# Two weight copies on TensorE, each made three times, ahead of the stream of matmuls

## The chip, the cores and the metric

One core of a Trainium2 chip. The time is the device time of one execution in microseconds; medians are given with the lowest and highest run. The profile's span is about 1.7 us shorter than that time. Only one core ran, so there is no second die to compare with; all timed runs used here are classed as fast, except the one single look (`pauses`), whose state is unknown.

## The reference, cut to what matters

```python
H = W = 384; C = 384; k = 1
x: (1, 384, 384, 384) bf16, dw: (1, 1, 384) bf16, pw: (384, 384) bf16
out = x * dw[0, 0]                          # k = 1: a scale per channel
return einsum('bhwc,cd->bhwd', out, pw)     # 147456 x 384 times 384 x 384
```

The scale is folded into the weights: `w_r = diag(dw) pw`, made once on the chip, and then one long product.

## The kernel before: the parts concerned

In the head, TensorE runs filler matmuls of zeros (`idle_work`), then makes the scaled and reordered weights. For each 128-row block `k` and half `r` it multiplies `pw_n` by a scaled selection matrix into PSUM (a pair of 64-row matmuls, `v` = 0, 1); ScalarE or VectorE copies each result to `w_r` in SBUF. I call such a pair "the copy (k, r)". Then comes the stream: 288 supertiles of 512 positions and 48 matmuls. VectorE transposes the input into `T`; each supertile uses four PSUM banks, and ScalarE copies them to `O`.

```python
idle_work(1)                              # 4 matmuls of zeros; idle_work(3) comes earlier
for k in range(3):
    if k < 2:
        nc.tensor.wait_ge(s_pw[k], 16)    # weights landed
    nc.tensor.wait_ge(s_sw, k + 1)
    for r in range(2):
        if k == 2:
            nc.tensor.wait_ge(*w_done[r]) # these PSUM banks are read out
        for v in range(2):
            mm = nc.tensor.matmul(PS[(k + 1) % 2][:, 2 * r + v, :D],
                lhsT=sel_w[64 * v : 64 * v + 64, k, r, :, :]...,
                rhs=pw_n[64 * v : 64 * v + 64, k, :],
                start=True, stop=True, tile_position=(64 * v, 0))
        mm.then_inc(s_w)
with nc.tensor.Fori(0, NS // 2, 1) as it:  # the stream
    ...                                    # first matmul waits for the third ScalarE copy of w_r
# ... cut
for t, (g, i, off, first, L) in enumerate(chunks):   # one queue for loads and stores
    todo.append((g_end[g - NR] if g >= NR else -1, load_x, t))
    todo.append((first + L + 1, store, t))
```

## Time and profile before

| | before |
|---|---|
| time, three runs | 576.89 us (576.73 to 577.27) |
| TensorE busy | 568.2 us, 99% of the span |
| stream starts | 6.47 us |
| one stream matmul, first supertile / rest of the run | 519 / 321 ns |
| first copy of outputs, last copy of outputs start | 10.54, 570.50 us |
| VectorE, ScalarE busy | 88%, 73% |

It is read from the end backwards: TensorE holds the chain, its stream has no idle time after the start, so the time is the start of the stream, plus the stream, plus a tail of stores. The lines themselves are in the prediction.

### The profile page before, as it was taken

What the parts mean: (1) busy time and instruction counts of PE and PEld (TensorE: products, weight loads), DVE (VectorE), ACT (ScalarE), POOL (GpSimd) and SP (SyncE); (2) the same over time, 40 slices, a digit from 0 to 9 for tenths busy, and PEclk for the clock granted to TensorE, in tenths of its full rate; (3) what the DMA queues carried; (4) which work ended last, traced back from release to release, by engine and by line L of the source; (5) the groups of instructions that cost most, each with busy time, mean ns of one, the idle gap of its engine ahead of it and who ended that gap; (6) DMA issues with size and microseconds to landing.
All of it is one profiled execution on the core that took longest, in us unless ns stands there. A gap on an engine that the chain in (4) does not pass through costs nothing.

```text
span 575.2 us, 29676 instructions
## 1 busy us (share of the span) xinstructions
PE 568.2 (99%) x13855; PEld 386.4 (67%) x13855; DVE 507.4 (88%) x583; ACT 418.8 (73%) x296; POOL 0.9 (0%) x8
## 2 busy tenths in 40 slices
PE   8999999999999999999999999999999999999996
PEld 4666666666666666666666666666666666666664
DVE  6889888988898889888988898889888988898884
ACT  5777777777777777777777777777777777777775
POOL 0000000000000000000000000000000000000000
PEclk9999999999999999999999999999999999999999
DMA  8999999999999999999999999999999999994996
GB/s 346 425 399 415 436 411 429 426 419 386 383 436 397 383 392 426 399 394 398 427 404 385 400 431 387 388 421 420 385 394 420 399 394 401 413 400 169 416 385 240
DMA packets 25928, 226.88 MB, mean 394 GB/s; under 512 B 1213, under 2 KB 5694, under 8 KB 22078
## 3 DMA queue, kind: packets, MB, share of 16 engines
q1 hardware_dynamic: 25916, 226.79, 98.0%
q14 instruction: 9, 0.07, 0.0%
q8 instruction: 1, 0.02, 0.0%
q10 hardware_dynamic: 2, 0.00, 0.0%
HBM read 113.54 MB, written 113.25 MB: 394 GB/s over the span
## 4 chain that ended last, share of the span: by engine, by line
PE 98%; ACT 1%; DMA 0%; DVE 0%; issue 0%; POOL 0%; POOLq 0%; SPq 0%
PE ps L167 97%; DMA out_dram<-O 0%; ACT w_r L271 0%; ACT O L307 0%; PE ps L184 0%; DVE O L304 0%; PE ps L216 0%; DVE sel_w L286 0%; POOL zero L232 0%; DVE dw_f L283 0%; POOL warm L231 0%; PE ps L199 0%; POOLq L337 0%; SPq L100 0%
## 5 line engine op out<-in xcount | busy, mean ns | idle before, releaser
L167 PE MATMUL ps<-w_r,T 32*128 32x384 bf16 x13824 | 564.0, 322 | 0.5 <-ACT w_r L271 0.5
L258 DVE STREAM_TRANSPOSE T<-X 128x384 uint32<-128x384 uint32 x576 | 504.2, 876 | 57.9 <-PE ps L167 1.2
L307 ACT CAST O<-ps 128x1536 bf16<-128x1536 f32 x288 | 413.6, 1436 | 149.9 <-PE ps L167 149.9
L167 PEld LDWEIGHTS ps<-w_r,T 32*128 32x128 bf16 x13824 | 385.1, 93 | 179.4 <-issue 0.9
L271 ACT CAST w_r<-ps 128x768 bf16<-128x768 f32 x5 | 3.6, 820 | 1.0 <-PE ps L216 1.0
L304 DVE CAST O<-ps 128x768 bf16<-128x768 f32 x1 | 1.0, 958 | 3.0 <-DMA out_dram<-O 3.0
L184 PE MATMUL ps<-zero 32*128 32x384 bf16 x16 | 1.8, 494 | 1.4 <-POOL zero L232 1.4
L216 PE MATMUL ps<-pw_n,sel_w 64*128 64x384 bf16 x12 | 2.4, 507 | 0.3 <-DVE sel_w L286 0.3
L244 ACT ACT_TABLE_LOAD x1 | 1.3, 1283 | 1.5 <-SPq L100 1.5
L216 PEld LDWEIGHTS ps<-pw_n,sel_w 64*128 64x128 bf16 x12 | 0.7, 109 | 2.0 <-DMA pw_n<-in_pw_dram 1.0
L276 DVE TENSOR_REDUCE sel<-eye 128x64 f32<-128x128 bf16 x1 | 0.3, 290 | 1.8 <-POOL eye L234 1.8
L184 PEld LDWEIGHTS ps<-zero 32*128 32x128 bf16 x16 | 0.5, 99 | 2.0 <-issue 2.0
L271 DVE CAST w_r<-ps 128x768 bf16<-128x768 f32 x1 | 1.0, 958 | 0.5 <-PE ps L216 0.5
L286 DVE TENSOR_SCALAR sel_w<-sel,dw_f 128x256 bf16<-128x256 f32 x3 | 0.9, 351 | 0.0
L283 DVE COPY dw_f<-ps 128x3 f32<-128x3 f32 x1 | 0.2, 160 | 0.8 <-PE ps L199 0.8
L199 PEld LDWEIGHTS ps<-ones,dw_row 1*128 1x128 bf16 x3 | 0.2, 99 | 0.2 <-issue 0.2
L234 POOL TENSOR_SCALAR_AFFINE_SELECT eye<-ones 128x128 bf16<-128x128 bf16 x1 | 0.3, 292 | 0.1
L244 ACT COPY warm<-warm 128x1 f32<-128x1 f32 x2 | 0.3, 189 | 0.0
L232 POOL MEMSET zero<- 128x192 uint32 x1 | 0.3, 258 | 0.0
L199 PE MATMUL ps<-ones,dw_row 1*128 1x1 bf16 x3 | 0.2, 160 | 0.0
L233 POOL MEMSET ones<- 128x128 bf16 x1 | 0.2, 204 | 0.0
L326 POOL MEMSET const-bfloat16-1.0<- 128x1 bf16 x1 | 0.1, 102 | 0.0
(4 smaller groups left out, 0.4 us busy)
## 6 DMA issues: line engine op xcount, KB each, us to landing
X<-in_x_dram SPq DMA_DIRECT2D x26, 3840.0 KB, 20.9
out_dram<-O SPq DMA_DIRECT2D x26, 3840.0 KB, 26.9
X<-in_x_dram SPq DMA_DIRECT2D x2, 1536.0 KB, 16.6
out_dram<-O SPq DMA_DIRECT2D x2, 1536.0 KB, 13.2
X<-in_x_dram SPq DMA_DIRECT2D x3, 768.0 KB, 7.3
out_dram<-O SPq DMA_DIRECT2D x3, 768.0 KB, 11.4
X<-in_x_dram SPq DMA_DIRECT2D x1, 2304.0 KB, 18.7
out_dram<-O SPq DMA_DIRECT2D x1, 2304.0 KB, 11.0
```

The costliest lines, as they stand in the source:

```text
L167: mm = nc.tensor.matmul(PS[s][:, q, :D], lhsT=Ts[s][32 * q : 32 * q + 32, b, par::2], rhs=w_r[32 * q : 32 * q + 32, b, par, :], start=(b, ...
L184: nc.tensor.matmul(PS[0][:, i, :D], lhsT=zero[32 * i : 32 * i + 32, 0:P], rhs=zero[32 * i : 32 * i + 32, :], start=True, stop=True, tile_p ...
L199: mm = nc.tensor.matmul(PS[1][:, 0, D + k : D + k + 1], lhsT=dw_row[:, P * k : P * k + P], rhs=ones[0:1, 0:1], start=True, stop=True,)
L216: mm = nc.tensor.matmul(PS[(k + 1) % 2][:, 2 * r + v, :D], lhsT=sel_w[64 * v : 64 * v + 64, k, r, :, :].rearrange("p q w -> p (q w)"), rhs ...
L232: nc.gpsimd.memset(zero[:].bitcast(U32), 0).then_inc(s_zero)
L234: nc.gpsimd.affine_select(out=eye[:], in_=ones[:], pattern=[[-1, P]], compare_op=mybir.AluOpType.is_equal, fill=0.0, base=0, channel_multi ...
L244: c = nc.scalar.copy(warm[:, s + 1 : s + 2], warm[:, 0:1])
L258: ins = nc.vector.transpose(out=Tw[:, 3 * h : 3 * h + 3], in_=Xw[:, :, j, 96 * h : 96 * h + 96].rearrange("p k (b w) -> p b k w", w=32),)
L271: o = nc.vector.tensor_copy(out, in_) if e == 0 else nc.scalar.copy(out, in_)
L286: nc.vector.tensor_scalar_mul(sel_w[:, k], sel[:].unsqueeze(2).to_broadcast([P, 2, 4, 32]), dw_f[:, k : k + 1]).then_inc(s_sw)
L304: e = nc.vector.tensor_copy(Ov[:, nq:4, j, :], PS[s][:, nq:4, :D])
L307: a = nc.scalar.copy(Ov[:, 0:nq, j, :], PS[s][:, 0:nq, :D])
```

## The change

The intent, as I read it, is to keep TensorE busy up to the first matmul of the stream. The copies (1, 1) and (2, 0) are issued three times. Each repeat writes the same product to the same banks again; the semaphore is raised after the last.

```diff
         idle_work(1)
+        times = {(1, 1): 3, (2, 0): 3}
         for k in range(3):
...
-                for v in range(2):
+
+                for v in [0, 1] * times.get((k, r), 1):
                     mm = nc.tensor.matmul(
```

## The prediction

> **What bounds the kernel now.** I first read part 1 and the chain that ended last (part 4), to see which engine sets the end.

> ```profile
> span 575.2 us, 29676 instructions
> PE 568.2 (99%) x13855; PEld 386.4 (67%) x13855; DVE 507.4 (88%) x583; ACT 418.8 (73%) x296; POOL 0.9 (0%) x8
> ...
> PE 98%; ACT 1%; DMA 0%; DVE 0%; issue 0%; POOL 0%; POOLq 0%; SPq 0%
> ...
> L167 PE MATMUL ps<-w_r,T 32*128 32x384 bf16 x13824 | 564.0, 322 | 0.5 <-ACT w_r L271 0.5
> ...
> PEclk9999999999999999999999999999999999999999
> ```

> TensorE carries 98% of the chain. Its 13,824 stream matmuls (line 167: 288 supertiles of 48) had only 0.5 us of idle time before them, all at the start of the stream. So only three things can shorten this kernel: an earlier start of the stream, a higher rate in it, or a shorter end. The row of granted clock reads 9 everywhere, so by it no rate is left to win. But a slice is 14.4 us; I therefore read the head in order of time, and then the duration of single stream matmuls in short windows.

> The head, TensorE and then ScalarE in the timeline (start us, us, what):

> ```profile
> 2.75 0.51 PE L184 MATMUL ps<-zero 32*128 32x384 bf16 x4
> 3.58 2.38 PE L216 MATMUL ps<-pw_n,sel_w 64*128 64x384 bf16 x12 [0.33 <-DVE sel_w L286]
> 6.47 1.79 PE L167 MATMUL ps<-w_r,T 32*128 32x384 bf16 x20 [0.51 <-ACT w_r L271]
> ```

> ```profile
> 4.12 3.61 ACT L271 CAST w_r<-ps 128x768 bf16<-128x768 f32 x5 [1.05 <-PE ps L216]
> ...
> 10.54 1.44 ACT L307 CAST O<-ps 128x1536 bf16<-128x1536 f32 x1 [2.81 <-PE ps L167]
> 12.81 1.44 ACT L307 CAST O<-ps 128x1536 bf16<-128x1536 f32 x1 [0.83 <-PE ps L167]
> 14.76 1.44 ACT L307 CAST O<-ps 128x1536 bf16<-128x1536 f32 x1 [0.51 <-PE ps L167]
> 16.71 1.44 ACT L307 CAST O<-ps 128x1536 bf16<-128x1536 f32 x1 [0.51 <-PE ps L167]
> ```

> The stream starts at 6.47, after a gap of 0.51 us in which TensorE waited for the third ScalarE copy of w_r. Each ScalarE copy of an output follows the end of a supertile. So supertile 0 took from 6.47 to about 10.52, 4.05 us; supertile 1 took 2.27; the later ones 1.95. The first ran at half rate. Groups of stream matmuls in four windows (6.4 to 10.5, 10.5 to 11, 11 to 11.25, 11.25 to 11.5) show when that ended, by the mean ns of one:

> ```profile
> L167 PE MATMUL ps<-w_r,T 32*128 32x384 bf16 x52 | 4.3, 519 | 0.5 <-ACT w_r L271 0.5
> ...
> L167 PE MATMUL ps<-w_r,T 32*128 32x384 bf16 x12 | 1.0, 469 | 0.0
> ...
> L167 PE MATMUL ps<-w_r,T 32*128 32x384 bf16 x12 | 0.9, 402 | 0.0
> ...
> L167 PE MATMUL ps<-w_r,T 32*128 32x384 bf16 x16 | 0.9, 332 | 0.0
> ```

> 519 ns falls to the 321 of the rest of the run at about 11.1 us. The other route agrees: supertile 1 is 2.27 - 1.95 = 0.32 us too long, which at half rate is 0.64 us of slow clock after 10.5. So the first 4.6 us of the stream run at half speed, though the granted-clock column says 1.00 there. As a check: 288 x 1.95 = 561.6; plus the start, 6.47; plus half of the slow stretch, (11.1 - 6.47)/2 = 2.3; together 570.4. The trace has the last copies of outputs starting at 570.50. The sum closes, and gives the rule used below: **the end moves by half of (start of the stream + moment at which the clock opens)**.

> [...] The window 4.3 to 7.7 is the one with the 0.51 us gap in it; 7.7 to 11.1 has none. No row of this trace shows a boundary itself. [...]

> **The change part by part.** Nothing is removed or moved; the listing by engine shows 4 more matmuls into each of the two PSUM tiles, and otherwise the same instructions in the same order on every engine. In the code each half-block r of weight block k is a pair of 64-row matmuls on different rows of the array. The pair (1,1) and the pair (2,0) are now each issued three times: 8 matmuls more. A pair costs 0.32 us cold.
> - Before: pairs start at 3.58, 3.90, 4.22, 4.54, then wait for copies out of PSUM: by the weight loads' timeline the fifth goes at about 5.05 and the sixth at 5.47. The last ends at 5.96. Then comes the gap to 6.47.
> - After: (1,1) runs at 4.54, 4.86, 5.18 and ends at 5.18 + 0.52 = 5.70, against 5.06 before. (2,0) runs at 5.50, 5.82, 6.14; (2,1) at 6.46. Both waits for copies (ScalarE's first ends at 4.92, VectorE's at 5.40) are over by then. The stream can issue at 6.78.
> - ScalarE's third copy reads what (1,1) wrote. It started at about 5.52 (the five start 0.70 apart) and now starts at about 5.72, ending at 6.52, plus 0.14 as before: 6.66. That is earlier than 6.78, so TensorE's own order is the later limit. **The start moves from 6.47 to 6.78: +0.31 us**, of the 8 x 0.16 = 1.28 us of added work; the rest lies in the two short waits and the 0.51 us gap.
> - The last two ScalarE copies end at about 7.5 and 8.2, against 7.73. With a fast clock from 7.7 the stream asks for them at steps 32 and 40 of the first supertile, about 8.5 and 8.9. Hidden.
> - The gain: TensorE is now busy without a break from 3.58 on. If the window 4.3 to 7.7 then counts as busy, the clock opens at 7.7 and not at 11.1. Half of (6.78 + 7.7) is 7.24, half of (6.47 + 11.1) is 8.79: **1.55 us less**.
> 576.89 - 1.55 = 575.34.

> **The rivals.**
> 1. The gate does not move: the window was short of activity for another reason, or the gate asks for longer. Then only the delay is left, halved, as the delayed start spends less time slow: +0.31/2 = +0.16, 577.05. For it: the earlier filler matmuls (from 1.43 on) did not open the gate either. Against it: they too were followed by a gap, 0.33 us.
> 2. The gate counts from the start of an unbroken run: 11.1 - 6.47 = 4.6 us from 6.47, so from 3.58 it opens at 8.2. Half of (6.78 + 8.2) is 7.49: -1.3, 575.6. If the window's phase differs between runs, the opening lies anywhere in 7.0 to 10.4, and the mean gain is near 1.2, with the times spread more widely. Against that phase: three runs of before lie within 0.54 us.
> 3. Data becomes the bound after a faster start. The input group of 3.84 MB first used by supertile 10 landed, by issue and time to landing, near 24.1 us. VectorE wanted it at about 25.5, and would want it at 23.9. That is 0.2 us short, but its tiles are needed on TensorE only some 2.9 us after that, and two transposes take 1.75, so about a microsecond is left. The one wait for input in the trace, 0.58 us at 8.94, stays where it is: supertile 2, which it feeds, starts only at about 11.15. From then on every input is a buffer ahead, as its load waits for the buffer, not the buffer for it. I expect nothing from this.
> 4. The stream's start slips more than I reckon, if a repeated pair must wait for its own weight load (0.10 to 0.15 us): up to +0.5 us of start, +0.25 of time, but still an unbroken run.

> **Range and chances.** I give the earlier opening about 3 in 4, with 575.3 to 575.6 as its centre, and the unmoved gate 1 in 4, at 577.0. The point is 575.5, a little above the best case. Repeats of before differ by 0.5 us, so the range is 574.8 to 577.1, which holds both outcomes. Two per cent is 11.5 us; nothing in the head is that large (the whole slow stretch costs 2.3), so faster and slower get one chance in a hundred each.

> **What the changed profile would show.** Twenty matmuls of the weight-copy row, running without a gap from 3.58 to 6.98. The stream's start at 6.8 (6.6 to 7.0). No idle time before it, in place of 0.51. The fall from 519 to 321 ns at 7.7 to 8.2, and not at 11.1. The first output copy near 9.2, not at 10.54, and the third 3.9 us after the first. The period stays 1.95. The prediction is wrong if the stream matmuls stay at 519 ns until 11, if TensorE has idle time in front of supertiles 2 to 11, or if the period changes.

The sum: half of (6.78 + 7.7) against half of (6.47 + 11.1) is 1.55 us, and 576.89 - 1.55 = 575.34. But the 7.7 in it, like the 4.3 and the 7.0 to 10.4 of rival 2, rests on a step of 3.4 us between possible openings (11.1 - 3.4 = 7.7), which the trace of before alone does not show. It is the author's estimate; the step itself was measured later, as 3.413 us (next section). The 0.32 us of a pair is what the trace shows (pairs at 3.58, 3.90, 4.22, 4.54).

## The result, and the profile after

The changed kernel took 575.61 us (575.24 to 576.30, six runs), against 577.07 (576.05 to 578.24, six runs) for the kernel before beside it. The ratio is 0.9976, with a 95% interval of 0.9963 to 0.9989: faster, and within 2%. (A ratio is the mean time of one kernel's runs over that of the other's of the same rounds, so it is not quite the ratio of the medians.) The outputs are right.

The stream's row in the page of the changed kernel, with no idle time before it:

```profile
L167 PE MATMUL ps<-w_r,T 32*128 32x384 bf16 x13824 | 562.2, 321 | 0.0
```

The head of the changed kernel, TensorE and then ScalarE, in order of time (start us, us, what):

```profile
2.74 0.51 PE L184 MATMUL ps<-zero 32*128 32x384 bf16 x4
3.58 3.70 PE L218 MATMUL ps<-pw_n,sel_w 64*128 64x384 bf16 x20 [0.33 <-DVE sel_w L288]
7.21 9.03 PE L167 MATMUL ps<-w_r,T 32*128 32x384 bf16 x208
```

```profile
9.80 1.44 ACT L309 CAST O<-ps 128x1536 bf16<-128x1536 f32 x1 [1.30 <-PE ps L167]
11.75 1.44 ACT L309 CAST O<-ps 128x1536 bf16<-128x1536 f32 x1 [0.51 <-PE ps L167]
13.70 1.44 ACT L309 CAST O<-ps 128x1536 bf16<-128x1536 f32 x1 [0.51 <-PE ps L167]
...
569.45 0.80 ACT L309 CAST O<-ps 128x768 bf16<-128x768 f32 x1 [0.51 <-PE ps L167]
```

The last copy of outputs in the trace of before, for comparison:

```profile
570.50 0.80 ACT L307 CAST O<-ps 128x768 bf16<-128x768 f32 x1 [0.51 <-PE ps L167]
```

Twenty matmuls of the copies now run into the stream. Although the stream starts 0.74 us later than before, its first supertile is copied out 0.74 us earlier (9.80 against 10.54). The second follows 1.95 us after the first, where before it took 2.27. The groups of stream matmuls from 7.5 to 8, 8 to 8.25 and 8.25 to 8.5 us show the clock opening near 8.1, where before it was 11.0:

```profile
L167 PE MATMUL ps<-w_r,T 32*128 32x384 bf16 x12 | 1.1, 489 | 0.0
...
L167 PE MATMUL ps<-w_r,T 32*128 32x384 bf16 x12 | 0.9, 431 | 0.0
...
L167 PE MATMUL ps<-w_r,T 32*128 32x384 bf16 x16 | 0.9, 353 | 0.0
```

After that TensorE shows no further difference: the last copy of outputs starts at 569.45, not 570.50 (1.05 earlier), and the span ends 4.7 us after it in both traces.

**A better instrument.** Besides its rows, each trace keeps a record of changes of the granted clock. In the trace of before it holds one full-speed stretch, from 11.00 us on, 563.199 us long; in that of the changed kernel one from 8.08 us, 566.612 us long. They differ by 3.413 us, and are 165.00 and 166.00 times 3.4133 us; the openings in `pauses`, below, lie whole multiples of the same step apart. A stretch of this length is called a window here. The record of before starts with its first change, at 11.00, and ahead of it the row of granted clock shows full speed: 1.00 from 6.4 to 10.5 us, where one matmul took 519 ns. After a stop, in `pauses`, the row has 0.50 from 97.7 to 103 us beside 516 to 522 ns, and 1.00 from 104 us on beside 321. From here on "opening" is this moment.

### The profile page after: what moved, and what is told of

It reads as the page before. It is cut to its first block, busy times and chain, and to the rows that moved or that the text cites. A ratio compares the mean times of both kernels' runs of the same rounds, so it can differ in the third digit from the quotient of the medians.

```text
span 574.1 us, 29692 instructions
## 1 busy us (share of the span) xinstructions
PE 567.5 (99%) x13863; PEld 334.3 (58%) x13863; DVE 508.2 (89%) x583; ACT 419.1 (73%) x296; POOL 0.9 (0%) x8
## 4 chain that ended last, share of the span: by engine, by line
PE 98%; DMA 1%; ACT 0%; DVE 0%; SPq 0%; issue 0%
PE ps L167 97%; DMA pw_n<-in_pw_dram 1%; PE ps L218 0%; DMA out_dram<-O 0%; ACT O L309 0%; DVE O L306 0%; SPq L132 0%; SPq L339 0%; SPq L100 0%
## 5 line engine op out<-in xcount | busy, mean ns | idle before, releaser
L167 PE MATMUL ps<-w_r,T 32*128 32x384 bf16 x13824 | 562.2, 321 | 0.0
L167 PEld LDWEIGHTS ps<-w_r,T 32*128 32x128 bf16 x13824 | 332.5, 93 | 229.9 <-issue 1.0
L218 PE MATMUL ps<-pw_n,sel_w 64*128 64x384 bf16 x20 | 3.6, 518 | 0.5 <-DVE sel_w L288 0.3
L184 PE MATMUL ps<-zero 32*128 32x384 bf16 x16 | 1.8, 493 | 1.4 <-POOL zero L234 1.4
L184 PEld LDWEIGHTS ps<-zero 32*128 32x128 bf16 x16 | 0.5, 99 | 2.0 <-issue 2.0
## 6 DMA issues: line engine op xcount, KB each, us to landing
out_dram<-O SPq DMA_DIRECT2D x2, 1536.0 KB, 13.8
out_dram<-O SPq DMA_DIRECT2D x1, 2304.0 KB, 11.3
```

What stands on the lines that cost most here:

```text
L167: mm = nc.tensor.matmul(PS[s][:, q, :D], lhsT=Ts[s][32 * q : 32 * q + 32, b, par::2], rhs=w_r[32 * q : 32 * q + 32, b, par, :], start=(b, ...
L184: nc.tensor.matmul(PS[0][:, i, :D], lhsT=zero[32 * i : 32 * i + 32, 0:P], rhs=zero[32 * i : 32 * i + 32, :], start=True, stop=True, tile_p ...
L218: mm = nc.tensor.matmul(PS[(k + 1) % 2][:, 2 * r + v, :D], lhsT=sel_w[64 * v : 64 * v + 64, k, r, :, :].rearrange("p q w -> p (q w)"), rhs ...
```

## The experiments

The theories, as the expectations name them. A: the clock opens at the end of a window of fixed length (the 3.413 us above) and free phase that TensorE kept busy. B: it opens a fixed time after an unbroken run began. C: the amount of work ahead of the stream counts, not its place. D: the later start itself helps. E: zeros do not count. F, formed later: some runs end late because of the order of transfers. The three sets of experiments ran on three chips (11, 5 and 4), each beside runs of the kernel before, so each is compared with those.

What the traces of all kernels showed; "end" is the span's end after the start of the last copy of outputs:

| trace | stream starts | clock opens | last copy starts | end | this run, us |
|---|---|---|---|---|---|
| before | 6.47 | 11.00 | 570.50 | +4.7 | 576.9 |
| changed, first | 7.21 | 8.08 | 569.45 | +4.7 | 575.9 |
| after_again | 6.90 | 6.96 | 568.74 | +4.7 | 575.2 |
| wrong_place | 7.68 | 6.58 | 569.51 | +4.7 | 575.9 |
| late_idle | 8.54 | 13.19 | 572.63 | +4.7 | 579.0 |
| early_too | 6.75 | 6.53 | 568.58 | +4.7 | 575.0 |
| first_only | 6.68 | 5.80 | 568.51 | +6.9 | 577.1 |
| second_only | 6.47 | 8.18 | 569.12 | +9.9 | 580.8 |
| dense | 6.64 | 6.74 | 568.50 | +7.0 | 577.2 |
| before_sf | 6.55 | 10.60 | 570.35 | +5.9 | 577.9 |
| after_sf | 6.97 | 8.04 | 569.85 | +6.4 | 578.0 |
| early_sf | 7.09 | 7.51 | 569.10 | +6.1 | 577.0 |
| dense_sf | 6.87 | 6.64 | 569.01 | +6.0 | 576.7 |

The rule of the prediction can be tried on all of them: last copy = 561.8 + half of (start + opening), or 561.8 + start where the clock opened before the start (561.8 is fitted to these traces; 288 x 1.95 is 561.6). It holds to 0.04 us in eleven of the thirteen. The two others, after_sf and dense_sf, are 0.54 and 0.34 late; both show a wait of TensorE in the stream, 0.38 us at 27.15 and 0.14 at 9.0, which is part of it. The wait in after_sf is rival 3 of the prediction: supertile 10 starts there, and VectorE had waited 2.38 us for its input (VectorE, then TensorE):

```profile
26.57 2.95 DVE L261 STREAM_TRANSPOSE T<-X 128x384 uint32<-128x384 uint32 x4 [2.38 <-DMA X<-in_x_dram]
27.53 12.70 PE L168 MATMUL ps<-w_r,T 32*128 32x384 bf16 x308 [0.38 <-issue]
```

In the two other traces with the changed head VectorE waited there too (0.54 us in the first, 1.70 in after_again), but TensorE did not.

### The changed kernel again

> The changed kernel once more, unaltered, to see how its head varies. In its first trace the second part of the weights landed at 4.49 us (3.97 in the trace of before), the stream started at 7.21 and its matmuls fell from 519 to 321 ns at about 8.2. Theory A (the clock opens at the end of a window of about 3.4 us of fixed length but free phase that TensorE kept busy from end to end): the fall comes anywhere from 3.4 to 6.8 us after the unbroken run began (3.6 to 4.5 us), so 7.0 to 11.3, and may move by more than a microsecond against the first trace. Theory B (it opens a fixed 4.6 us after the unbroken run began): the fall is at 8.2 to 9.1 again. Both: about 575.6 us, ratio to before 0.9975.

No edit. 575.25 us (575.12 to 575.77, five runs), ratio 0.9967 (0.9953 to 0.9981). The clock opened at 6.96, 1.1 us earlier than in the first trace of the same kernel, and 3.4 us after the copies began at 3.58. Theory B asked for 8.2 or later: it falls. In both traces the window before the opening (4.67 to 8.08, 3.55 to 6.96) is one that TensorE kept busy.

### The same work in another place

```diff
-times = {(1, 1): 3, (2, 0): 3}
+times = {(0, 0): 3, (0, 1): 3}
```

> The same 8 extra matmuls, but as repeats of the first two copies (0,0) and (0,1), where they do not bridge the gap ahead of the stream. By the timeline of before, all later copies slip by about 1.2 us, the gap of 0.6 us before the stream stays, and the stream starts near 7.7. If what counts is an unbroken run up to the stream (theories A and B), the fall from 519 to 321 ns moves later, to about 12.3 (4.6 after 7.7), and the time becomes 576.9 + half of (1.2 + 1.2) = 578.1. If it is the amount of matmul work ahead of the stream that counts, whatever its place (theory C), the fall comes near 8.2 as with the change, and the time is 576.9 + half of (1.2 - 2.9) = 576.0.

577.86 us (575.91 to 577.99, five runs), ratio 1.0007 (0.9992 to 1.0022): no gain, from the same eight matmuls. The head in its trace:

```profile
3.58 3.49 PE L218 MATMUL ps<-pw_n,sel_w 64*128 64x384 bf16 x20 [0.33 <-DVE sel_w L288]
7.68 4.57 PE L167 MATMUL ps<-w_r,T 32*128 32x384 bf16 x108 [0.61 <-ACT w_r L273]
```

The stream starts at 7.68 after a gap of 0.61, as reckoned. Three of five runs are near the 578.1 of theory A (577.86 to 577.99); one is at 576.97, between the theories. The profiled one, at 575.91, was the fortunate one: its clock opened at 6.58, before the gap. I had not reckoned with that: the moved repeats make a run of their own, from 3.58 to 6.64. It is shorter than a window, but the window from 3.17 to 6.58 held, besides it, only the gap from 3.25 to 3.58. Theory C, which wants 576.0 in every run, does not fit.

### A late start without work

```diff
+nc.tensor.wait_ge(s_t[0][1], 1)           # before the stream of the kernel before
 with nc.tensor.Fori(0, NS // 2, 1) as it:
```

> The kernel before without any repeat, but TensorE waits for the second transposed half before it starts the stream, so that the stream starts late (about 7.0 in place of 6.47, as late as with the change) after an idle gap in place of repeats. If the activity is what opens the clock early (A, B, C), there is no gain: the fall stays 3.4 to 6.8 us after the start, 10.4 to 13.8, and the time is 577.1 to 577.6, 0.2 to 0.5 over before. If the later start itself is what helped (theory D: data and transposes further ahead when it starts), the time falls towards 575.6.

578.49 us (577.32 to 579.08, five runs), ratio 1.0016 (1.0000 to 1.0032). In the trace the first input landed late (6.55), so the stream started at 8.54 and not at 7.0, and four of the five times are above the expected 577.1 to 577.6; the clock opened at 13.19, 4.65 after the start. A later start alone brings no gain (the interval begins at 1.0000); theory D falls. With its own start and opening the rule gives 572.67 for the last copy; measured 572.63.

### More filler early

```diff
-idle_work(1)
+idle_work(2)                              # with the change
```

> The change, and one more round of four filler matmuls of zeros in the gap from 3.26 to 3.58 us, so that TensorE is busy almost without a break from 1.43 us on. Theory A: the fall comes between 4.9 and 8.2 us, so most often before the stream starts (about 7): the whole stream is fast, and the time is up to half of 8.2 - 7.0 = 0.6 us below the change, 575.0. Theory B: it falls at 1.43 + 4.6 = 6.0, the same time. If instead zeros do not count as activity (theory E), nothing changes against the change: fall at about 8.2, 575.6.

575.17 us (574.98 to 577.05, six runs), ratio 0.9975 (0.9958 to 0.9992). The clock opened at 6.53, ahead of the stream's start at 6.75; four runs lie at 575.0 to 575.2. But two lie at 577, where theory A, with an opening by 8.2, cannot put them. That was the first sign of another effect. On theory E this is not decisive: the changed kernel itself opened at 6.96 without this filler. The trace of first_only, below, speaks against E: its clock opened at 5.80, and the window before that (from 2.39) held filler and one-column matmuls up to 3.25 and a gap to 3.58. Without these 0.87 us it would have been idle for about 1.2 us, more than the 0.51 us with which a window of before failed.

### The clock's grid in one run

```diff
-with nc.tensor.Fori(0, NS // 2, 1) as it:
+cuts = [0, 20, 45, 75, 110, NS // 2]
+for c in range(5):
+    if c:
+        nc.tensor.wait_ge(s_go, ...)       # after 10 to 13 memsets on GpSimd
+    with nc.tensor.Fori(cuts[c], cuts[c + 1], 1) as it:
```

> The kernel before, with TensorE stopped four times in the stream (after supertiles 40, 90, 150 and 220) for some 12 to 16 us each, while GpSimd fills a scratch tile. It is slower on purpose, by some 60 us; it measures the clock. After each stop the stream begins again at half rate and one sees when it turns fast. Theory A (windows of fixed length and free phase): the five moments of opening in this one trace lie on one grid, at whole multiples of about 3.41 us from each other, to within 0.15 us, and each lies 3.0 to 6.8 us after the stream restarts. Theory B (a fixed time after the restart): each lies the same time after its restart, and no grid fits. In three earlier traces the time from the start of the unbroken run to the opening was 4.6, 4.6 and 3.3 us, which speaks against B already.

636.29 us, one run, slower on purpose. The stream in the timeline of TensorE, with the stops:

```profile
6.47 80.63 PE L169 MATMUL ps<-w_r,T 32*128 32x384 bf16 x1920 [0.51 <-ACT w_r L284]
97.68 100.60 PE L169 MATMUL ps<-w_r,T 32*128 32x384 bf16 x2400 [10.57 <-POOL slow L255]
209.83 118.66 PE L169 MATMUL ps<-w_r,T 32*128 32x384 bf16 x2880 [11.55 <-POOL slow L255]
341.08 139.08 PE L169 MATMUL ps<-w_r,T 32*128 32x384 bf16 x3360 [12.59 <-POOL slow L255]
493.76 135.63 PE L169 MATMUL ps<-w_r,T 32*128 32x384 bf16 x3264 [13.60 <-POOL slow L255]
```

The clock record gives openings at 11.50, 103.66, 212.89, 346.01 and 499.61 us: 5.0, 6.0, 3.1, 4.9 and 5.9 us after the starts in the lines. No fixed delay fits, which is a second blow to B. Their distances are 27.00, 32.00, 39.00 and 45.00 times the 3.4133 us of the two stretches above, and the full-speed stretches are 23, 29, 35, 40 and 39 windows long, to 0.01. That is theory A's grid: fixed in a run, and with another phase in each run (11.00, 10.60 and 11.50 in three traces with the head of before). The third opening came 3.06 us after its start, less than a window: this window held 0.35 us of idle time, so one need not be busy from end to end.

### One repeat at a time

```diff
-times = {(1, 1): 3, (2, 0): 3}
+times = {(1, 1): 3}          # first_only;    second_only: {(2, 0): 3}
```

> Only the copy (1,1) three times. It fills the short gaps ahead of the last two copies, and by the timeline the last copy then ends its issue at 6.14, with ScalarE's third copy ready at 6.5 and the stream at 6.66: a gap in issue of 0.5 us is left, or more where the input lands late, near the one of before (0.67). Theory A: a window that holds this gap (15 per cent of 3.4 us) mostly fails, so most runs stay near before, 576.5 to 577.2, and some fall to 575.5. If both repeats add equally to a sum of work (theory C), it lies half way, 576.3, in every run.

577.05 us (574.91 to 577.13, six runs), ratio 0.9979 (0.9953 to 1.0006). The number fits the expectation, but the trace says that it does so for another reason. The clock opened at 5.80, before the gap and the stream, and the last copy of outputs started at 568.51, 2 us ahead of before. Then the run ended late. This is the list of issues near the end (size of each, median us to landing), first of after_again (issues from 568.3 to 569.6 us), then of first_only (the same stretch):

```profile
out_dram<-O SPq DMA_DIRECT2D x1, 384.0 KB, 2.3
```

```profile
out_dram<-O SPq DMA_DIRECT2D x2, 384.0 KB, 4.1
```

The last stores took 4.1 us to land, not 2.3, and the gain of the head was lost in the tail. The run at 574.91 is probably this kernel without that; it has no trace.

> Only the copy (2,0) three times. By the timeline a gap in issue of 0.2 us is left ahead of (2,0) (ScalarE's first copy ends at 4.92), then it runs unbroken from 5.05 to 6.33, and the stream starts at about 6.47 as before: the gap of 0.67 us ahead of the stream shrinks to about 0.2. Theory A: windows now lose about 0.2 to 0.4 us, 6 to 12 per cent, and wrong_place opened with about that much, so most runs gain: 575.2 to 575.8, as the change or 0.1 better, as the start does not slip.

576.53 us (574.96 to 580.80, six runs), ratio 0.9984 (0.9948 to 1.0019). Three runs are at 574.96 to 575.05, better than the changed kernel's median; three are at 578.0 to 580.8. In the trace of the slowest the head is good (opening at 8.18, last copy at 569.12), and the last stores took 7.3 us to land. Of the two repeats, then, either alone can be enough for the clock: by its trace each opened it earlier than before, and, as one trace each proves little where the grid differs from run to run, five of their twelve runs (574.91 to 575.50) lie below every one of the 37 runs of before (576.05 and more). Which gains more often stays open, because the late ends cover it.

### A denser head

```diff
-with nc.tensor.Fori(0, n, 1) as _:       # in idle_work; and idle_work(2) for idle_work(1)
+for _ in range(n):
-times = {(1, 1): 3, (2, 0): 3}
+times = {(0, 1): 2, (1, 1): 2, (2, 0): 3}
```

> A version meant to beat both: the filler of zeros without its loop (no gaps between its rounds) and one round more, one repeat moved from (1,1) to (0,1) so that a late second part of the weights finds TensorE busy, 8 extra copies as in the change. TensorE is busy from 1.43 us to the start of the stream with only the three one-column matmuls at 2.6 in between. Theory A: every phase gives an opening by 8.3, most before the stream starts at 6.8; 574.9 to 575.4 in every run, without runs near 577 as early_too had in two of six. Theory E (zeros do not count): as the change, 575.2 to 576.3.

576.64 us (576.14 to 578.26, six runs), ratio 0.9988 (0.9962 to 1.0014), a miss by 1.5 us. The head did what was planned (opening at 6.74, last copy at 568.50, the earliest of all), but the span ended 7.0 us after it.

What goes before a late end is seen on the sync engine, whose one queue issues loads and stores in order. Its timeline from 505 to 531 us, first of after_again, then of first_only:

```profile
511.16 13.31 SPq L113 DMA_DIRECT2D X<-in_x_dram  x5
524.51 4.41 SPq L128 DMA_DIRECT2D out_dram<-O  x1
```

```profile
510.93 17.77 SPq L113 DMA_DIRECT2D X<-in_x_dram  x5
528.74 4.41 SPq L128 DMA_DIRECT2D out_dram<-O  x1
```

The engine sits in the issue of the last five loads for 13.3 us, or for 17.8; in second_only it was 21.3. The store behind them is ready by about 516 (the next experiment lets it out at 515.9 to 517.2), but goes out only when they are issued. The loads held longest are the last two, of 768-byte rows: 6.60 and 5.03 us in after_again, 15.17 and 4.42 in second_only (the 6.6 and 15.2 of the expectation below). Meanwhile the DMA engines are mostly free: their busy share is 0.34 and 0.42 from 520 to 530 us in after_again, and 0.19 and 0.26 from 525 to 535 in second_only, against about 1.0 up to 515. So nothing shows the DMA engines at their limit while the issue holds. In the long cases the DMA engines are then busy to the end. That made theory F.

### The store ahead of the last loads

```diff
+late = 2.5 if g == len(groups) - 1 else 0
-todo.append((g_end[g - NR] if g >= NR else -1, load_x, t))
+todo.append((g_end[g - NR] + late if g >= NR else -1, load_x, t))
```

> The kernel before, with one change in the order of the queue of transfers: the loads of the last group (two of long rows, three of 768-byte rows) are issued after the store of supertiles 250 to 259, not ahead of it. Theory F (some runs end late because the sync engine sits in the issue of those loads, 6.6 us in a good trace and 15.2 in a bad one, and the store behind them starts late, so that the last stores land late): the late ends go, and the last store always lands as in good traces, the span ending about 4.7 us after the last copy of outputs starts. Times 576.5 to 577.6, as the head varies, without the 578 to 581 that before shows in some runs. If the late ends come from elsewhere (slow memory in those runs), the spread stays.

> The changed kernel with the same reordering. Theories A and F: 575.0 to 575.8 by where the clock's grid lies, so the difference to before_sf is the clock alone, 1.2 to 2.0 us. If the gain of the change came partly from the end of the run, the difference is smaller than 1.

> early_too (the change, and a second round of zero filler at 2.75 us) with the same reordering: the two of six runs at 577 should go, 574.9 to 575.3 in all. A candidate to beat both kernels.

> dense with the same reordering. All six runs of dense were at 576.1 to 578.3 though its trace had the fastest head (first outputs copied from 8.85 us on); its last stores landed 4.6 us after issue, not 2.3. Theory F: now 574.8 to 575.3 in all runs, over 1.3 us less than dense. If the slow ends of dense have another cause, they stay near 576.5.

Five runs each, ratio to the kernel before, beside which they ran (576.74 us, 576.11 to 577.37): before_sf 577.92 (577.71 to 578.86), 1.0023 (1.0009 to 1.0036); after_sf 576.99 (576.38 to 577.97), 1.0001 (0.9987 to 1.0015); early_sf 576.61 (576.09 to 576.98), 0.9995 (0.9981 to 1.0009); dense_sf 576.61 (576.03 to 576.77), 0.9993 (0.9979 to 1.0007). As a remedy this failed in every one. Two lines of the sync engine in after_sf show why:

```profile
516.72 0.40 SPq L128 DMA_DIRECT2D out_dram<-O  x1
517.16 21.48 SPq L113 DMA_DIRECT2D X<-in_x_dram  x5
538.69 32.55 SPq L128 DMA_DIRECT2D out_dram<-O  x8
```

The store went out at 516.72, 8 us earlier than in after_again. But the loads behind it now held the engine for 21.5 us, and the next store, which in after_again went out at 535.11, waited until 538.69. The wait was moved from one store to the next. All four traces end 5.9 to 6.4 us after the last copy, where good traces have 4.7. So the runs show that the order in this queue sets part of the end (before_sf is 1.2 us slower than before beside it), and in the traces without reordering a long hold and a late end go together: 13.2 to 15.1 us with +4.7, 17.8 and 17.9 with +6.9 and +7.0, 21.3 with +9.9. That the waiting store is the cause is argued and not shown, since no run took the wait away. Nor do they show why the loads hold the engine longer in some runs of one and the same kernel; this stays open. One run of before took 581.35 us and may be such a case; it has no trace.

Within this set the change is still worth something, but how much is not settled: after_sf over before_sf is 1.0001/1.0023, 0.22% or 1.3 us, while the medians are only 0.93 us apart. The expectation had 1.2 to 2.0 for the clock alone and under 1 if part of the gain came from the end of the run; these five runs each do not decide between the two.

No version beat the changed kernel clearly: early_too's median is 0.08 us below that of after_again, with two runs of six 1.7 us and more above its other four.

## Why the prediction was right, point by point

- **Outcome.** 575.5 was forecast, 575.61 measured, and all eleven runs of the changed kernel (575.12 to 576.30) lie in the range. That the number is so close is partly luck: the gain of the two traces alone differs by 0.7 us, with the grid and the landings of the run.
- **The mechanism, an earlier opening: right.** The opening came at 8.08 and 6.96 (8.04 in after_sf, with the same head), not at 11.00. It was the busy stretch, not the later start (late_idle), and not the mere amount of work (wrong_place). Rival 1, an unmoved gate, did not occur in these three traces.
- **The moment of opening: right as an estimate, wrong as a number.** I gave 7.7, a step of 3.4 us back from the opening in one trace. A trace fixes the grid for its own run only. Rival 2's first form, a fixed delay, is refuted; its second, a phase that differs, is what runs show. I had held three close runs of before against it; the openings in three traces with that head lie at 10.60 to 11.50.
- **The start of the stream: too early.** 6.78 was forecast, 6.90 and 7.21 measured. The first 0.12 of this is within the amount of rival 4, but did not come by its way: in after_again the repeated pairs follow each other at 0.32 us, with no wait for their own weights. The last pair starts at about 6.44 and the stream's first weight load only at 6.90, where 0.32 of streaming would allow 6.76; the runs do not show why. The rest in the first trace is landing: the second part of the weights landed at 4.49 (3.97 before) and the first input at 6.24 (by 5.33 before), and the first transpose ended at 7.12. The term was sized on one trace's landings. The first copy of outputs came at 9.80 and 9.09; 9.2 was forecast.
- **The sum.** With the measured start and opening, half of (7.21 + 8.08) is 7.65, against half of (6.47 + 11.00) = 8.74: 1.09 us. The last copies of outputs are 1.05 apart. In after_again the rule gives 1.80 and the trace 1.76. The forecast 1.55 lies between, since a late start and an earlier opening than 8.08 err in opposite directions.
- **Rival 3, data as the bound: dismissed too soon.** I looked for it in the head only. In the changed kernel it cost nothing in the two traces, but in after_sf, with the same head, it did: the input of supertile 10 was put near 24.1 us, VectorE got it at 24.87, 25.33 and 26.57 in the three traces, and in the last the microsecond that I had left was used up and TensorE waited 0.38 us. And the end of a run can be set by the last stores, in this kernel and in the one before, and in the traces of first_only and dense it took back the whole gain of the head (2.0 us each).

## What to carry to other kernels

Where a kernel is bound by one stream on TensorE, look at the duration of single matmuls in its first ten microseconds: here the slow clock cost some 2 us of 577, and a few matmuls repeated into a gap of half a microsecond won more than half of that back. In these traces what counted was that a window of 3.413 us be busy nearly throughout, wherever it fell (at most 0.35 us of visible idle time in those that opened the clock, 0.41 and 0.51 in two that did not), so an effect of this kind must be judged over several runs and by the opening in each trace. And before a gain is credited or denied to a change in the head, the tail of the same trace has to be read: first_only had the expected time for a reason that its theory did not contain.
